# A bias row with the heads innermost, written from two partitions and read back in long runs

## The chip, the cores and the metric

One NeuronCore of a Trainium2 chip runs the whole program. The metric is the device time in microseconds of one execution; lower is better. Engines are named as in the profile: PE (TensorE), ACT (ScalarE), DVE (VectorE), POOL (GpSimd), SP (SyncE, which only issues DMAs). ACT and POOL issue DMAs as well.

## The reference

Attention with a relative position bias over batch 8, 8 heads, 576 positions and head size 64, followed by a mixture of eight low-rank adapters of which each row uses its two best.

```python
scores = scale * q @ k.T                     # scale = 1/8
n = abs(pos[:, None] - pos[None, :])
bucket = n if n < 16 else 16 + int(log(n/16)/log(8) * 15), at most 31
scores += bias_table[bucket]                 # table of 32 buckets x 8 heads
attn = softmax(scores); x = attn @ v         # rows of 8 heads x 64
logits = x @ w_gate; two best experts, softmax over the two
out = x + sum over both of w * (x @ A[e]) @ B[e]
```

The bias depends on the distance alone. From distance 128 on it is constant, and a constant falls out of the softmax. So a row of 512 numbers per head, indexed by signed distance, holds all of it, and every tile of bias is a shifted copy of this row.

## The kernel before, in words

**Tiling.** The work goes in 32 pairs of heads (8 batches x 4 pairs, pair hp holds heads hp and hp+4). A pair has five steps g: four of 128 keys against 512 queries for both heads (PE writes 128x1024 scores, ACT takes the exponential, L375 and L396), and a fifth for the 64 tail positions (L381). The first 512 positions are split as position = 4 p + j. After its steps a pair is multiplied by v (pv, L426), divided (recip and norm) and written to x. The mixture of a batch is spread over the slots of the next two batches; the tuple MIX says in which slot each of its parts is issued.

**Order.** Nothing is scheduled automatically: the order of each engine is the order of the calls. At the start the steps are reordered by START: the twelve main steps of pairs 0 to 2 come first, then their three tail steps, since these need the bias tile B. OPS lists, by step, what else is issued: ckq and pkq cast q and k, T transposes them, M makes a bias table for a pair, b multiplies the probabilities of a step by it, cv casts v, ts scores the tails, pv and rn finish a pair. SPQ, POOLQ and POOLQ2 are the orders of the SP and POOL queues at the start.

**The bias.** The table (32 x 8) is loaded by two DMAs with the heads on 8 partitions (L69 to L73). POOL subtracts the last bucket and scales (L212); gg holds per head the row of logarithms and its exponential (512 each, L208 and L236). It is filled with copies by POOL and ACT (L225 to L235), one for each bucket of several distances. ACT writes gg to a DRAM buffer g_d (L238). From there it is read back with a shift for each partition:
- Mr (L243, load_bias at L247): the exponential, for the main steps. Partition 32 j + t begins at 4 t + j; 8 heads x 384 numbers, in four DMAs on SP, one for each j. band_table (L286) turns a pair's part round into M, read at a step of -4 numbers; band_of (L402) multiplies the probabilities by it on DVE.
- MHr (L262) and Br (L256): the logarithm, for the tail steps, in two and four DMAs on POOL. tail_bias (L290) makes B4 and BT of them on POOL, which PE adds to the scores through an identity (L357, L389, L391).

All of this happens while ACT already takes exponentials, which need no bias; M and B are needed when the first pair is finished. At most eight DMAs of the hardware queues have a semaphore of their own: the next one on SP waits until the DMA eight before it has landed.

cv(0), the first cast of v, needs all four groups of v (16 DMAs of 64 KB in SPQ). On DVE it stands after M(1) and four b.

Of the kernel before, what the change touches and what calls it, by code (L numbers as in the profile page):

```python
# [10 lines left out]
FP32 = mybir.dt.float32  # L11
BF16 = mybir.dt.bfloat16
AX = mybir.AxisListType
ALU = mybir.AluOpType
ACT = mybir.ActivationFunctionType
# [12 lines left out]
def kernel(  # L28
# [14 lines left out]
    nc = tc.nc  # L43
    B, H, S, D = q.shape
    NB = bias_table.shape[0]
# [4 lines left out]
    HP = H // 2  # L50
    D1 = D + 1
    scale = 1.0 / float(np.sqrt(D))
    S4 = 512
    MW = 384
# [3 lines left out]
    cp = ctx.enter_context(tc.tile_pool(name="const", bufs=1))  # L58
    ldp = ctx.enter_context(tc.tile_pool(name="loads", bufs=2))
# [5 lines left out]
    op = ctx.enter_context(tc.tile_pool(name="outs", bufs=2))  # L65
    scp = ctx.enter_context(tc.tile_pool(name="sc_ps", bufs=2, space=PSUM))
    acp = ctx.enter_context(tc.tile_pool(name="acc_ps", bufs=4, space=PSUM))

    btT = cp.tile([H, NB], FP32, tag="btT")  # L69
    for e in range(2):  # L70
        (nc.gpsimd if e else nc.scalar).dma_start(
            out=btT.rearrange("(c e) b -> e c b", e=2)[e],
            in_=bias_table.rearrange("b (e c) -> e c b", e=2)[e])  # L73
    warm = cp.tile([128, 1], FP32, tag="warm")
    nc.vector.memset(warm, 0.0)
    fill = cp.tile([128, 512], BF16, tag="fill")
    nc.vector.memset(fill, 1.0)
    nc.scalar.activation(warm, warm, ACT.Exp)
    ident = cp.tile([128, 128], BF16, tag="ident")
    make_identity(nc, ident)  # L80

    START = ((0, 0), (0, 1), (0, 2), (0, 3), (1, 0), (1, 1), (1, 2), (1, 3), (2, 0), (2, 1),
             (2, 2), (2, 3), (0, 4), (1, 4), (2, 4))
    SPQ = (('v', 0), ('v', 1), ('M', 0, 8), ('v', 2), ('v', 3), ('kq', 0, 3), ('kq', 1, 0),
           ('kq', 1, 1), ('kq', 1, 2), ('kq', 1, 3), ('v1', 0), ('v1', 1), ('v1', 2),
           ('v1', 3))
    POOLQ = (('tl', 0, 0), ('tl', 0, 1), ('tl', 1, 0), ('tl', 1, 1), ('MH', 0), ('MH', 1),
             ('Br', 0), ('Br', 1), ('Br', 2), ('Br', 3))
    POOLQ2 = (('vt', 0), ('vt', 1), ('B', 0), ('B', 1), ('B', 2))
    OPS = {0: (('ckq', 1), ('T', 1)),  # L90
           3: (('ckq', 2),),
           4: (('T', 2),),
# [3 lines left out]
           8: (('M', 0),),  # L96
           9: (('b', 0, 0), ('b', 0, 1)),
           10: (('M', 1), ('b', 0, 2), ('b', 0, 3), ('ts', 0), ('pkq', 4, 0)),
           11: (('cv', 0), ('b', 1, 0), ('b', 1, 1)),
           12: (('M', 2), ('b', 1, 2), ('b', 1, 3), ('T', 3), ('pkq', 4, 1)),  # L100
           13: (('cv', 1), ('b', 2, 0), ('b', 2, 1), ('pv', 0, 0), ('pv', 0, 1), ('pv', 0, 2),
                ('rn', 0, 0)),
# [3 lines left out]
           17: (('pv', 2, 0), ('pv', 2, 1), ('pv', 2, 2), ('rn', 2, 0)),  # L106
           18: (('cv', 3), ('tt', 1), ('pv', 2, 3), ('pv', 2, 4), ('rn', 2, 1))}
    LAST = ((2, 'pv', 0), (2, 'pv', 1), (1, 'eh', 7), (1, 'pv', 2), (1, 'pv', 3))

    def keep_busy(n, cols=512):  # L110
        ps = acp.tile([128, 512], FP32, name="fl", tag="acc")
        for _ in range(n):
            nc.tensor.matmul(ps[:, :cols], lhsT=fill[:, 0:128], rhs=fill[:, :cols],
                             start=True, stop=True, skip_group_check=True)

    class Recorder:

# [12 lines left out]
    dve = Recorder(nc.vector)  # L130
# [9 lines left out]
    kfs, vns, vfs = {}, [], {}  # L140
# [11 lines left out]
    def load_v(b, js):  # L152
        if b not in vfs:
            vfs[b] = ldp.tile([128, 4, H, D], FP32, name="vf", tag="vf")
        vr = v[b, :, :S4, :].rearrange("h (t p j) d -> j t p h d", t=4, j=4)
        return [nc.sync.dma_start(out=vfs[b][j * 32:(j + 1) * 32, t], in_=vr[j, t])
                for j in js for t in range(4)]
# [3 lines left out]
    tls, vts = [], []  # L161
    for i in range(2):
        tl = cp.tile([128, 2, HP, 128], BF16, name=f"tl{i}", tag=f"tl{i}")
        tls.append(tl)
        vt = cp.tile([128, HP, 2 * D1], BF16, name=f"vt{i}", tag=f"vt{i}")
# [4 lines left out]
    def load_tail(b, w, e):  # L170
        sr = (k, q, v)[w][b, :, S4:, :].rearrange("(e c) p d -> e p c d", e=2)
        s = slice(e * 64, (e + 1) * 64)
        o = (tls[b % 2][s, w, :, s] if w < 2 else
             vts[b % 2][s, :, e * D1:e * D1 + D])
        nc.gpsimd.dma_start(out=o, in_=sr[e])  # L175
# [16 lines left out]
    def v_ones(eng, vt):  # L192
        eng.memset(vt[0:64, :, D:D1], 1.0)
        eng.memset(vt[64:128, :, 2 * D + 1:2 * D1], 1.0)
# [5 lines left out]
    for t in tls[:1] + vts[:1]:  # L200
# [4 lines left out]


    C = 255
    gg = cp.tile([H, 2, 512], BF16, tag="gg")  # L208
    g_sb = gg[:, 0]
    nc.gpsimd.memset(g_sb, 0.0)  # L210
    bsub = cp.tile([H, NB], FP32, tag="bsub")
    nc.gpsimd.tensor_scalar(bsub, btT, btT[:, NB - 1:NB], 1.0 / scale,  # L212
                      op0=ALU.subtract, op1=ALU.mult)
    buckets = [_bucket(d, NB) for d in range(256)]
    lo = 0
    runs = []
    for d in range(1, 129):
        if d == 128 or buckets[d] != buckets[lo]:
            runs.append((buckets[lo], lo, d))
            lo = d  # L220
    assert all(x == NB - 1 for x in buckets[128:])
    nsm = 0
    while runs[nsm][0] == nsm and runs[nsm][2] == nsm + 1:
        nsm += 1
    nc.gpsimd.tensor_copy(g_sb[:, C:C + nsm], bsub[:, :nsm])  # L225
    nc.gpsimd.tensor_copy(
        g_sb[:, C - nsm + 1:C],
        bass.AP(tensor=bsub.tensor, offset=bsub.offset + nsm - 1,
                ap=[bsub.ap[0], [-1, nsm - 1]]))
    for bv, lo, hi in runs[nsm:]:  # L230
        n = hi - lo
        dst = bass.AP(tensor=g_sb.tensor, offset=g_sb.offset + C - hi + 1,
                      ap=[g_sb.ap[0], [hi - 1 + lo, 2], [1, n]])
        (nc.scalar.copy if bv % 3 else nc.gpsimd.tensor_copy)(
            dst, bsub[:, bv:bv + 1].unsqueeze(2).to_broadcast((H, 2, n)))  # L235
    nc.scalar.activation(gg[:, 1], g_sb, ACT.Exp, scale=scale)  # L236
    g_d = nc.dram_tensor("g_d", (H, 2, 512), BF16, kind="Internal")
    nc.scalar.dma_start(out=g_d.ap(), in_=gg)  # L238
    cast_kq(0, 0, dve)
    cast_kq(0, 1, dve)  # L240
    gt = g_d.ap()

    Mr = cp.tile([128, H, MW], BF16, tag="Mr")  # L243
    MHr = cp.tile([128, HP, 192], BF16, tag="MHr")
    Br = cp.tile([128, H, 64], BF16, tag="Br")

    def load_bias(h0, h1):  # L247
        for j in range(4):
            nc.sync.dma_start(
                out=Mr[j * 32:(j + 1) * 32, h0:h1],  # L250
                in_=bass.AP(tensor=gt.tensor, offset=gt.offset + h0 * 1024 + 512 + j,
                            ap=[[4, 32], [1024, h1 - h0], [1, MW]]))

    alloc_kq(1)

    def load_br(j, eng):  # L256
        eng.dma_start(
            out=Br[j * 32:(j + 1) * 32],
            in_=bass.AP(tensor=gt.tensor, offset=gt.offset + 64 + j,
                        ap=[[4, 32], [1024, H], [1, 64]]))  # L260

    def load_mh(e, eng):  # L262
        eng.dma_start(
            out=MHr[e * 64:(e + 1) * 64],
            in_=bass.AP(tensor=gt.tensor, offset=gt.offset + e * 1024 + 192,
                        ap=[[1, 64], [2048, HP], [1, 192]]))

    for f, *a in SPQ:
        {"v": lambda j: load_v(0, (j,)), "M": load_bias, "kq": load_kq,
         "v1": lambda j: load_v(1, (j,)), "Br": lambda j: load_br(j, nc.sync),  # L270
         "MH": lambda e: load_mh(e, nc.sync)}[f](*a)
    for f, *a in POOLQ:
        {"tl": lambda w, e: load_tail(0, w, e), "Br": lambda j: load_br(j, nc.gpsimd),
         "MH": lambda e: load_mh(e, nc.gpsimd)}[f](*a)

# [4 lines left out]
    def at(t, off, *dims):  # L282
        return bass.AP(tensor=t.tensor, offset=t.offset + off,
                       ap=[t.ap[0]] + [list(d) for d in dims])

    def band_table(hp):  # L286
        dve.tensor_copy(M[:, 2 * hp:2 * hp + 2],
                        at(Mr, 2 * hp * MW + MW - 1, (MW, 2), (-1, 4), (-4, 96)))

    def tail_bias(n):  # L290
        if n == 0:
            return nc.gpsimd.tensor_copy(
                B4[:, :, 0:128].rearrange("p c (j u) -> p c j u", j=4),
                at(MHr, 191, (192, HP), (-1, 4), (-4, 32)))
        if n == 1:
            return nc.gpsimd.tensor_copy(BT.rearrange("p c (e t) -> p c e t", e=2),
                                         at(MHr, 63, (192, HP), (0, 2), (-1, 64)))
        nc.gpsimd.tensor_copy(  # L298
            B4[:, :, 128:256].rearrange("p c (e t) -> p c e t", e=2),
            at(Br, 63, (128, HP), (64, 2), (-1, 64)))  # L300

    for f, *a in POOLQ2:
        {"vt": lambda e: load_tail(0, 2, e), "B": tail_bias, "cv": cast_v}[f](*a)
    for t in tls[1:] + vts[1:]:
        nc.gpsimd.memset(t, 0.0)
    v_ones(nc.gpsimd, vts[1])
    nc.gpsimd.memset(vns[1][:, :, :, D:D1], 1.0)


    Ab = cp.tile([128, 4, ER], BF16, tag="Ab")  # L310
# [519 lines left out]
    def pool_kq(i, w):  # L830
# [2 lines left out]
    START_OPS = {  # L833
        "cv": lambda p: cast_v(p, dve), "cvp": cast_v, "M": band_table, "b": band_of,
        "tt": tail_transposes, "ts": tail_scores, "pv": pv, "rn": renorm, "T": transposes,
        "w": keep_busy, "vt": load_tail, "B": tail_bias,
        "ckq": lambda i: (cast_kq(i, 0, dve), cast_kq(i, 1, dve)), "pkq": pool_kq}

    MIX = (4, 9, 17, 19, 19, 19, 20, 20, 22, 24, 25, 27, 30, 32, 39)
    VSLOTS = ((), (5, 7, 9, 10), (5, 7, 8, 10), (8, 10, 12, 13))  # L840
    KQSLOTS = ((14, 16), (11, 13), (11, 13), ())
    TSLOTS = ((15, 16, 17, 18), (15, 16, 17, 18), (15, 16, 17, 18), (15, 16, 17, 18))
# [107 lines left out]
```

## Time and profile before

Three runs took 203.14, 203.54 and 206.69 us, median 203.54. The profiled execution took 202.09 us, of which the span of the profile is 200.3.

| | busy us | share of the span |
|---|---|---|
| PE | 176.4 | 88% |
| DVE | 164.0 | 82% |
| ACT | 165.7 | 83% |
| POOL | 101.0 | 50% |

| stage of the start | us from the span's start |
|---|---|
| table landed, POOL subtracts | 4.88 |
| first exponential of scores | 7.58 |
| gg to g_d issued by ACT, landed | 7.21, 10.63 |
| Mr issued on SP, first M table on DVE | 10.71 to 12.51, 17.91 |
| MHr and Br issued on POOL | 10.92 to 14.48 |
| B and BT made on POOL | 16.82, 17.40, 20.29 |
| v landed, cast on DVE | 22.80 |
| first multiplication by v on PE | 26.74 |

Lines of the profile name the engine, the line of the kernel, the operation and out<-in; in brackets stands the idle time of the engine before it and what ended that time. L126 is the helper through which all DVE instructions go, so these are told apart by the tile.

### The profile page before, as it was taken

What the parts mean: (1) busy time and instruction counts of PE and PEld (TensorE: products, weight loads), DVE (VectorE), ACT (ScalarE), POOL (GpSimd) and SP (SyncE); (2) the same over time, 40 slices, a digit from 0 to 9 for tenths busy, and PEclk for the clock granted to TensorE, in tenths of its full rate; (3) what the DMA queues carried; (4) which work ended last, traced back from release to release, by engine and by line L of the source; (5) the groups of instructions that cost most, each with busy time, mean ns of one, the idle gap of its engine ahead of it and who ended that gap; (6) DMA issues with size and microseconds to landing.
All of it is one profiled execution on the core that took longest, in us unless ns stands there. A gap on an engine that the chain in (4) does not pass through costs nothing.

```text
span 200.3 us, 6922 instructions
## 1 busy us (share of the span) xinstructions
PE 176.4 (88%) x2754; PEld 118.5 (59%) x2754; DVE 164.0 (82%) x446; ACT 165.7 (83%) x198; POOL 101.0 (50%) x184
## 2 busy tenths in 40 slices
PE   1785299899999999999999999999999999999980
PEld 0342177576666667766676666666666677567730
DVE  4515599999997998889988997999879987998680
ACT  2899337899979989898979898998799898999550
POOL 4783976598755457264735383446544342411000
PEclk9999759999999999999999999999999999999999
DMA  6999999899999988999999999999999946822176
GB/s 176 246 177 162 271 317 161 131 336 159 143 240 253 155 211 171 319 223 122 221 305 313 173 196 195 363 168 182 173 297 294 225 111 183 108 110 106 56 250 221
DMA packets 87060, 41.18 MB, mean 206 GB/s; under 512 B 66284, under 2 KB 83852, under 8 KB 87028
## 3 DMA queue, kind: packets, MB, share of 16 engines
q1 hardware_dynamic: 68512, 38.15, 80.2%
q0 software_dynamic: 18144, 2.18, 19.1%
q8 instruction: 21, 0.34, 0.7%
q10 hardware_dynamic: 372, 0.41, 0.7%
q14 instruction: 11, 0.09, 0.2%
HBM read 29.97 MB, written 9.45 MB: 197 GB/s over the span
## 4 chain that ended last, share of the span: by engine, by line
PE 65%; ACT 13%; DMA 9%; POOL 5%; issue 4%; DVE 0%; DVEq 0%; ACTq 0%; POOLq 0%
PE pv L426 16%; PE sc L375 15%; ACT p L396 11%; PE sc L381 8%; PE kqps L337 7%; PE zp L563 4%; DMA Br<-g_d 3%; PE dl L584 3%; DMA tl<-in_q_dram 2%; PE tps L346 2%; DMA g_d<-gg 2%; DMA btT<-in_bias_table_dram 2%; PE lp L519 1%; PE ztps L576 1%; PE tsc L355 1%
## 5 line engine op out<-in xcount | busy, mean ns | idle before, releaser
L396 ACT ACTIVATE p<-sc 128x1024 bf16<-128x1024 f32 x160 | 152.5, 1028 | 15.6 <-PE sc L381 10.5
L126 DVE TENSOR_TENSOR p<-p,M 128x512 bf16<-128x512 bf16 (+1 forms) x128 | 62.4, 509 | 0.1
L375 PE MATMUL sc<-kqT 64*128 64x512 bf16 x256 | 51.6, 402 | 7.6 <-ACT p L396 6.7
L426 PE MATMUL pv<-vn,p 128*128 128x65 bf16 x1240 | 57.6, 196 | 0.0
L426 PEld LDWEIGHTS <-p 128*128 128x128 bf16 x1364 | 48.9, 100 | 14.1 <-issue 9.3
L185 POOL CAST kqn<-qf 128x512 bf16<-128x512 f32 x29 | 18.1, 624 | 40.0 <-DVE rc L126 35.0
L126 DVE TENSOR_TENSOR x<-pv,rc 128x384 bf16<-128x384 f32 x64 | 29.0, 453 | 1.2
L185 POOL CAST kqn<-kf 128x512 bf16<-128x512 f32 x29 | 18.2, 629 | 22.6 <-DVE zT L126 6.3
L126 DVE COPY kqT<-kqps 128x1024 bf16<-128x1024 bf16 x32 | 22.0, 687 | 9.1 <-PE kqps L337 8.4
L337 PE MATMUL kqps<-ident,kqn 128*128 128x128 bf16 x256 | 21.9, 231 | 7.1 <-DVE kqn L126 4.5
L375 PEld LDWEIGHTS <-kqT 64*128 64x128 bf16 x256 | 12.9, 94 | 25.1 <-issue 17.9
L426 PE MATMUL pv<-vt,p 128*128 128x130 bf16 x124 | 27.4, 221 | 0.0
L337 PEld LDWEIGHTS <-kqn 128*128 128x128 bf16 x256 | 15.5, 102 | 15.4 <-issue 5.9
L189 POOL CAST vn<-vf 128x512 bf16<-128x512 f32 x28 | 19.3, 691 | 5.7 <-DVE rc L126 4.4
L126 DVE RECIPROCAL rc<-pv 128x6 f32<-128x6 f32 x64 | 11.6, 181 | 8.0 <-PE pv L426 7.1
L126 DVE TENSOR_TENSOR o<-dl,x 128x512 f32<-128x512 f32 x25 | 17.0, 680 | 0.4 <-PE dl L782 0.4
L381 PEld LDWEIGHTS <-kqT 128*128 128x128 bf16 x128 | 10.0, 99 | 7.6 <-issue 2.5
L381 PE MATMUL sc<-kqT,tlT 128*128 128x512 bf16 x32 | 12.3, 386 | 1.1 <-ACT p L396 1.0
L381 PE MATMUL sc<-tlT,kqT 128*128 128x128 bf16 x128 | 12.6, 221 | 0.0
L381 PE MATMUL sc<-B,ident 128*128 128x128 bf16 x64 | 9.1, 222 | 2.2 <-POOL B L298 2.2
L175 POOL DMA_DIRECT2D vt<-in_v_dram x16 | 10.1, 636 | 0.9 <-PE sc L375 0.9
L175 POOL DMA_DIRECT2D tl<-in_k_dram x16 | 9.9, 621 | 0.0
(123 smaller groups left out, 190.4 us busy)
## 6 DMA issues: line engine op xcount, KB each, us to landing
vf<-in_v_dram SPq DMA_DIRECT2D x128, 64.0 KB, 3.6
kf<-in_k_dram SPq DMA_DIRECT2D x6, 1024.0 KB, 6.8
qf<-in_q_dram SPq DMA_DIRECT2D x6, 1024.0 KB, 9.9
out_dram<-o SPq DMA_DIRECT2D x12, 512.0 KB, 5.6
kf<-in_k_dram SPq DMA_DIRECT2D x8, 256.0 KB, 4.9
qf<-in_q_dram SPq DMA_DIRECT2D x8, 256.0 KB, 4.9
out_dram<-o SPq DMA_DIRECT2D x7, 256.0 KB, 2.6
out_dram<-ot SPq DMA_DIRECT2D x7, 128.0 KB, 7.1
```

The lines of the kernel that those rows point to most:

```text
L126: self.last = f(*a, **kw)
L175: nc.gpsimd.dma_start(out=o, in_=sr[e])
L185: return (eng or nc.gpsimd).tensor_copy(o, s)
L189: return (eng or nc.gpsimd).tensor_copy(vns[b % 2][:, :, hp:H:HP, :D], vfs[b][:, :, hp:H:HP, :])
L337: nc.tensor.transpose(o, n[:, w, j], ident)
L346: nc.tensor.transpose(ps[:, w, c, :], tls[b % 2][:, w, c, :], ident)
L375: nc.tensor.matmul(sc[:, h * 512:(h + 1) * 512], lhsT=t[s, 0, g * 128:(g + 1) * 128], rhs=t[s, 1, :], start=True, stop=True)
L381: nc.tensor.matmul(o, lhsT=lhsT, rhs=rhs, start=start, stop=stop, skip_group_check=True)
L396: nc.scalar.activation(p, scs.pop(n), ACT.Exp, scale=scale)
L426: nc.tensor.matmul(o, lhsT=lhsT, rhs=rhs, start=start, stop=stop, skip_group_check=True)
L563: nc.tensor.matmul(zp[:, t - t0, :], lhsT=xT[:, 4 * t + c, :], rhs=Ab[:, c, :], start=(t == t0 and c == 0), stop=(c == 3), skip_group_chec ...
L584: nc.tensor.matmul(ps, lhsT=zT[:, t, :], rhs=Bb, start=True, stop=True)
```

## The change

The row is built with the heads innermost: gg is 512 distances x 8 heads, in 33 partitions of which 0 holds the logarithms and 32 the exponentials (1 to 31 repeat 0). The table is loaded once into 33 partitions, by one DMA on ACT. DVE does the subtraction, the scaling and the first two copies; POOL and ACT copy the buckets of several distances, the shorter on POOL. The far ends are filled by memsets, on POOL for partitions 0 to 31 and on DVE for 32. gg takes a buffer of the loads of v, which batch 1 uses later.

g_d is now two rows of 4096 numbers. Mr, MHr and Br come by one DMA each, whose runs are 384, 192 and 64 distances of all 8 heads: 6, 3 and 1 KB. MHr holds all eight heads and not four. M, B4 and BT are made of them by the same copies, which now step over the heads (by -32 or -8 numbers).

The orders change with it. On SP, M stands before the second group of v, and k and q of pair 3 before the third. On POOL, the memsets of the second buffers (ms) move from behind B to places between the DMAs, and the load of the v tails goes ahead of them. cv(0) moves behind b(1,0) and b(1,1). MIX moves five of its fifteen parts. A tile for filling matmuls, which nothing used, goes with its memset.

```diff
-    btT = cp.tile([H, NB], FP32, tag="btT")
-    for e in range(2):
-        (nc.gpsimd if e else nc.scalar).dma_start(
-            out=btT.rearrange("(c e) b -> e c b", e=2)[e],
-            in_=bias_table.rearrange("b (e c) -> e c b", e=2)[e])
+    bt = cp.tile([33, NB, H], FP32, tag="bt")
+    nc.scalar.dma_start(out=bt, in_=bass.AP(tensor=bias_table.tensor, offset=bias_table.offset,
+                                            ap=[[0, 33], [1, NB * H]]))
...
-    fill = cp.tile([128, 512], BF16, tag="fill")
-    nc.vector.memset(fill, 1.0)
...
-    SPQ = (('v', 0), ('v', 1), ('M', 0, 8), ('v', 2), ('v', 3), ('kq', 0, 3), ('kq', 1, 0),
+    SPQ = (('v', 0), ('M',), ('v', 1), ('kq', 0, 3), ('v', 2), ('v', 3), ('kq', 1, 0),
...
-    POOLQ = (('tl', 0, 0), ('tl', 0, 1), ('tl', 1, 0), ('tl', 1, 1), ('MH', 0), ('MH', 1),
-             ('Br', 0), ('Br', 1), ('Br', 2), ('Br', 3))
-    POOLQ2 = (('vt', 0), ('vt', 1), ('B', 0), ('B', 1), ('B', 2))
+    POOLQ = (('tl', 0, 0), ('tl', 0, 1), ('tl', 1, 0), ('tl', 1, 1), ('ms', 0), ('MH',),
+             ('Br',), ('vt', 0), ('vt', 1), ('ms', 1), ('ms', 2))
+    POOLQ2 = (('B', 0), ('B', 1), ('B', 2))
...
-           11: (('cv', 0), ('b', 1, 0), ('b', 1, 1)),
+           11: (('b', 1, 0), ('b', 1, 1), ('cv', 0)),
...
-    gg = cp.tile([H, 2, 512], BF16, tag="gg")
-    g_sb = gg[:, 0]
-    nc.gpsimd.memset(g_sb, 0.0)
-    bsub = cp.tile([H, NB], FP32, tag="bsub")
-    nc.gpsimd.tensor_scalar(bsub, btT, btT[:, NB - 1:NB], 1.0 / scale,
-                      op0=ALU.subtract, op1=ALU.mult)
+    NSPLIT = 8
+    gg = ldp.tile([33, 512, H], BF16, name="gg", tag="vf")
+    far = bass.AP(tensor=gg.tensor, offset=gg.offset,
+                  ap=[[gg.ap[0][0], 32], [383 * H, 2], [1, 129 * H]])
+    nc.gpsimd.memset(far, 0.0)
+    dve.memset(bass.AP(tensor=gg.tensor, offset=gg[32:33].offset,
+                       ap=[[gg.ap[0][0], 1], [383 * H, 2], [1, 129 * H]]), 1.0)
+    bd = cp.tile([33, NB, H], FP32, tag="bd")
+    tb = cp.tile([33, NB, H], BF16, tag="tb")
+    dve.tensor_tensor(bd, bt, bt[:, NB - 1:NB, :].to_broadcast((33, NB, H)), op=ALU.subtract)
+    nc.scalar.activation(tb[32:33], bd[32:33], ACT.Exp)
+    dve.tensor_scalar(tb[0:32], bd[0:32], 1.0 / scale, None, op0=ALU.mult)
...
+    dve.tensor_copy(gg[:, C:C + nsm], tb[:, :nsm])
...
-        (nc.scalar.copy if bv % 3 else nc.gpsimd.tensor_copy)(
-            dst, bsub[:, bv:bv + 1].unsqueeze(2).to_broadcast((H, 2, n)))
-    nc.scalar.activation(gg[:, 1], g_sb, ACT.Exp, scale=scale)
-    g_d = nc.dram_tensor("g_d", (H, 2, 512), BF16, kind="Internal")
-    nc.scalar.dma_start(out=g_d.ap(), in_=gg)
+        (nc.scalar.copy if n > NSPLIT else nc.gpsimd.tensor_copy)(dst, src)
+    G = 512 * H
+    g_d = nc.dram_tensor("g_d", (2, 4, G // 4), BF16, kind="Internal")
+    nc.scalar.dma_start(out=g_d.ap(), in_=bass.AP(
+        tensor=gg.tensor, offset=gg.offset,
+        ap=[[gg.ap[0][0] * 32, 2], [G // 4, 4], [1, G // 4]]))
...
-    def load_bias(h0, h1):
-        for j in range(4):
-            nc.sync.dma_start(
-                out=Mr[j * 32:(j + 1) * 32, h0:h1],
-                in_=bass.AP(tensor=gt.tensor, offset=gt.offset + h0 * 1024 + 512 + j,
-                            ap=[[4, 32], [1024, h1 - h0], [1, MW]]))
+    def load_bias(eng=nc.sync):
+        eng.dma_start(
+            out=Mr.rearrange("p x h -> p (x h)"),
+            in_=bass.AP(tensor=gt.tensor, offset=gt.offset + G,
+                        ap=[[H, 4], [4 * H, 32], [1, MW * H]]))
...
-    def load_br(j, eng):
+    def load_br(eng):
         eng.dma_start(
-            out=Br[j * 32:(j + 1) * 32],
-            in_=bass.AP(tensor=gt.tensor, offset=gt.offset + 64 + j,
-                        ap=[[4, 32], [1024, H], [1, 64]]))
-    def load_mh(e, eng):
+            out=Br.rearrange("p x h -> p (x h)"),
+            in_=bass.AP(tensor=gt.tensor, offset=gt.offset + 64 * H,
+                        ap=[[H, 4], [4 * H, 32], [1, 64 * H]]))
+    def load_mh(eng):
         eng.dma_start(
-            out=MHr[e * 64:(e + 1) * 64],
-            in_=bass.AP(tensor=gt.tensor, offset=gt.offset + e * 1024 + 192,
-                        ap=[[1, 64], [2048, HP], [1, 192]]))
+            out=MHr.rearrange("p x h -> p (x h)"),
+            in_=bass.AP(tensor=gt.tensor, offset=gt.offset + 192 * H,
+                        ap=[[HP, 2], [H, 64], [1, 192 * H]]))
...
     def band_table(hp):
         dve.tensor_copy(M[:, 2 * hp:2 * hp + 2],
-                        at(Mr, 2 * hp * MW + MW - 1, (MW, 2), (-1, 4), (-4, 96)))
+                        at(Mr, (MW - 1) * H + hp, (HP, 2), (-H, 4), (-4 * H, 96)))
...
-                at(MHr, 191, (192, HP), (-1, 4), (-4, 32)))
+                at(MHr, 191 * H, (1, HP), (-H, 4), (-4 * H, 32)))
...
-    MIX = (4, 9, 17, 19, 19, 19, 20, 20, 22, 24, 25, 27, 30, 32, 39)
+    MIX = (4, 10, 17, 19, 19, 20, 20, 22, 22, 24, 25, 27, 27, 32, 39)
```

## The prediction

> **What bounds the kernel now.** I read the page first. TensorE is busy 88% of the span, ScalarE 83%, VectorE 82%, so no engine is idle enough to blame; the 40 slices put the losses into the first 30 us, and only there does the change do much.
>
> ```profile
> span 200.3 us, 6922 instructions
> PE 176.4 (88%) x2754; PEld 118.5 (59%) x2754; DVE 164.0 (82%) x446; ACT 165.7 (83%) x198; POOL 101.0 (50%) x184
> ```
>
> Second, the windows (stretch, length, busy us of PE, PEld, DVE, ACT, POOL, then granted clock, DMA share, GB/s).
>
> ```profile
> 15.00:17.50 2.50, 1.25 (x8) 0.20 (x5) 0.65 (x1) 2.50 (x4) 1.42 (x4) 1.00 1.19 177
> 20.00:22.50 2.50, 0.77 (x8) 0.47 (x7) 0.74 (x2) 0.98 (x2) 2.21 (x3) 0.97 1.23 190
> 22.50:25.00 2.50, 0.61 (x4) 0.34 (x4) 2.19 (x4) 0.96 (x2) 2.35 (x7) 0.50 1.10 349
> 25.00:27.50 2.50, 2.23 (x24) 1.96 (x25) 2.50 (x4) 0.52 (x1) 1.60 (x3) 0.50 1.10 348
> 27.50:30.00 2.50, 2.50 (x41) 1.68 (x38) 2.46 (x6) 1.13 (x2) 1.99 (x4) 0.66 1.33 288
> ```
>
> Until 20 us ScalarE's exponentials set the pace. From 20 to 25 us TensorE and ScalarE both stand, and the clock falls to 0.50. From 25 us VectorE is full, until 37.5. So a change of this stage is worth what it moves on VectorE after 22 us. Third, the waits between 5 and 32 us, and the chain of waits (start, us, what).
>
> ```profile
> ACT p L396 <- PE sc L381: 5.1, 2, 3.5
> POOL B L298 <- DMA Br<-g_d: 2.3, 1, 2.3
> DVE M L126 <- DMA Mr<-g_d: 2.3, 1, 2.3
> PE sc L381 <- POOL B L298: 2.2, 1, 2.2
> DVE vn L126 <- DMA vf<-in_v_dram: 2.1, 1, 2.1
> ```
> ```profile
> 7.21 3.42 DMA g_d<-gg
> 13.88 6.20 DMA Br<-g_d
> 20.29 0.92 POOL B L298
> ```
>
> The bias row is written at 7.21, its copies arrive 13 us later, and B is ready at 21.2. But two things end late together. VectorE's own row is
>
> ```profile
> 22.80 0.43 DVE L126 CAST vn<-vf 128x512 bf16<-128x512 f32 x1 [2.06 <-DMA vf<-in_v_dram]
> 23.15 1.30 DVE L126 TENSOR_TENSOR p<-p,M 128x512 bf16<-128x512 bf16 x2
> 24.37 1.77 DVE L126 COPY M<-Mr 128x768 bf16<-128x768 bf16 x1
> 27.27 0.68 DVE L126 COPY kqT<-kqps 128x1024 bf16<-128x1024 bf16 x1
> 29.43 0.18 DVE L126 RECIPROCAL rc<-pv 128x6 f32<-128x6 f32 x1
> ```
>
> It waits for v at 22.80 and reaches the first division at 29.43. That instruction is my yardstick: what it is moved by, the rest of the full stretch is moved by.
>
> **The change, part by part.**
>
> *Building the row.* Removed: one table load from the POOL queue (0.89 us), the memset of fill (0.48 on VectorE), 8-row work on POOL and the exponential over 512 columns (0.63). Added on VectorE, in front of the first k cast: a memset of 2064 elements in one partition. Rows: 512 elements took 0.485 us, 4 took 0.062, so 0.83 ns each, 1.77 us, from 2.25 to 4.0. Then the subtraction and the scaling of 256 (by the 0.42 us cast of 512, some 0.3 each) and two copies, until about 5.2. The copies wait for POOL's memset and ScalarE's exponential, and behind them on VectorE stand the first k and q casts, for which TensorE waits: they stood at 3.44 and 4.59 and come at 5.2 and 5.6, so the first scores are some 1.0 us later, at about 8.0. ScalarE's first exponential stood at 7.58, held by issuing g_d, so it loses 0.45. ScalarE idles 1.53 us before 21.52 and 3.52 before 26.98: that idleness hides the 0.45. If both vanish, it counts in full. POOL now has ten copies of 48 to 128 elements; five took 0.74, and 512 elements cost 0.61 (B), so 10 x 0.13 + 0.8 = 2.1 us, from 4.9 to 7.0. g_d is issued at about 7.2 as before. It is now two rows of 8 KB: in the trace the 8-row write raises its semaphore by 8 arrivals, a 32-row load by 16, the 4-row table load from ScalarE's queue by 4. Two instead of eight writers: 0 to 0.5 us, I take 0.3, so g_d lands at 10.9 (10.63).
>
> *POOL.* Six DMAs for MHr and Br (2 x 0.63 + 4 x 0.60 = 3.7 us) become two (1.2); the memset of tl (0.95) goes ahead of them, those of vt and vn ahead of B. MHr is issued at about 11, when it was. The 4-row table load from POOL raised its semaphore by 16 arrivals, so I take POOL's loads as spread. Before, MHr landed 4.2 to 5.2 us after issue; after, about 15.5. The three B copies took 0.61 to 0.92 and read now at steps of 64, 16 and 16 bytes instead of 8, 2 and 2: at 0.92 each, B is ready at 18.3, ahead of the 19.8 at which TensorE gets there. The 2.2 us wait goes. What is late next is v and M.
>
> The skill's rule here (GPSIMD Engine Reference, Performance pitfalls) is half as much again for GpSimd reads at steps over 8 bytes; by it B would be ready at about 18.3 too, still hidden.
>
> *VectorE's M copies* read at 64 bytes instead of 8. No row has that step: between no change (0.55) and the 1.5 of the slowest B copy against the quickest (0.83). Two of four fall into the full stretch: 0 to 0.55, I take 0.3.
>
> *SP's queue.* M moves ahead of the second v row group, four DMAs become one (1.80 us of issue to 0.45), k/q of pair 3 ahead of v groups 2 and 3. SP has then only 4 v loads to issue before it waits for g_d, and is idle from 6.6 to 10.9 instead of 9.3 to 10.7; behind the wait stand 12 v loads and all of batch 1.
>
> *How quickly M arrives decides.* 768 KB in 6 KB runs; the page's rate while 1 KB runs flow alone is 348 GB/s (22 to 28 us), 2.3 us if all 16 engines share it. But its source pattern is 4 x 32 runs (outer loop of four), its destination 128 rows. The rows I have (arrivals 4, 8, 16 for outer loops of 4, 8, 32) fit "as many engines as the outer loop allows", and none has two different outer loops. On 4 engines: 196.6 KB each; at 348/16 = 21.8 GB/s it is 9.0 us, at the 4 KB packets of the out stores (159 ns) 7.6. So 2.3 to 9.0; I take four engines, since the smaller loop fits all rows, and 8.0.
>
> The skill speaks against the change in the same place (DMA: Bandwidth & Descriptors, Rules for kernel authors, "Use all 16 engines"): the slowest loop of either pattern caps the engines, so an outer size of 4 confines the copy to four. By that rule the sum is the 204.4 below; with all engines it is the 201.9 of the first rival.
>
> On four engines: issue 10.9, first packet 1.0 later as in the trace, 8.0, landing 0.95 after the last packet: 20.85 (17.9 now). In the built program the sixth v load after M waits for M's semaphore, so seven v loads are issued only from 20.85, 0.45 each, the last landing at least 2.1 later (the least v landing in the trace): 26.1. VectorE: cv 0.43, M 0.55, two p 0.95, kqT 0.69, cv 0.42, two p 0.90 (quiet rows: POOL's memsets and casts are out of the way) bring the first division to 30.05 against 29.43, +0.6. (The M tables and six p of pairs 0 and 1 fit between 20.85 and 25.) With 0.3 for the M step: +0.9.
>
> *MIX.* z moves from slot 20 to 22, away from the tail scores; one output from 30 to 27, beside another. ScalarE idles 5.7 us in six waits for the tail scores, VectorE 1.7 for the gate. The move may win up to 0.3 or lose 0.3 in each of six batches, since two 0.68 us additions now stand together on a VectorE 90% busy. I take 0.
>
> *Sum.* +0.9 on the profiled 202.09 us (span 200.3 and 1.8 around it) is 203.0; the median of the runs, 203.54, lies 1.45 above that execution, so 204.4.
>
> **The rivals.**
>
> *M spreads over 16 engines.* For it: 128 destination rows. M and MHr land by 15.5, k/q of pair 3 by 19, and v, the last in the queue, at 23.3 (12 loads x 0.62, k/q 1.5, from 14.2). The division comes at 27.5, -1.9, +0.3 for the step: 201.9. With MIX's best (-1.8) it would be 200.1. It ends on the other side of mine. It decides if M lands before about 18.
>
> *MHr is confined too,* to two engines (its source loop is 2 x 64), and shares them with M: 8 us each, 16 together, from 11.9 to 28. B is ready at 30 instead of 21.2. ScalarE's idle 5.0 us hides part: +4, 207.5; with engines of its own MHr lands at 21 and costs +1.5. Against it: the 16 arrivals of POOL's 4-row load. It decides once B is later than about 24.
>
> *The change does nothing:* v sets the end anyway, at 22.8 before and after, and only the M step and MIX are left: 203.5 plus or minus 1.
>
> **How the numbers follow.** Four engines for M 0.48, sixteen 0.28, MHr confined 0.14, nothing 0.10. The likeliest gives 204.4 us, its own range 202.9 to 206 (landing of v 25.5 to 27.5, MIX within 1). Of all, 8 in 10 lie between 200.9 and 207.4. About 2%, some 4 us, is what a measurement of this kernel tells from no change: below 199.5 lies a fifth of the sixteen-engine case and little else, 0.08; above 207.6 half of the confined case and a tail of mine, 0.14; the rest 0.78.
>
> **What would show it.** Right: M's first copy on VectorE at 20 or later with a wait for Mr, no wait of TensorE for B, the cast of v at about 26, the first division at 30. Mr landing under 5 us from issue says sixteen engines, MHr over 9 us says it is confined. First exponential near 8.0 and g_d issued near 7.2 check the row building. M copies over 0.9 us would make the step dearer than taken. The forecast is wrong if VectorE is not full from 25 us on, or if the idle share of TensorE between 60 and 180 us (116 of 120 busy now) changes by more than 2 us: then MIX did it.

## The result and the profile after

The changed kernel took 216.85, 219.49, 223.75 and 225.60 us, median 221.62, beside 203.57 for the kernel before on the same chip: 1.0725 times as long, 95% interval 1.0568 to 1.0881. It is slower; 204.4 was forecast, with 207.4 as the upper end. (The two longest runs were disturbed and are left out of the ratio; they are in the median.) The profiled execution took 219.49 us.

The page of the changed kernel: in microseconds every engine is busy about as long as before, only the span is longer. The 40 slices are 5.4 us each. PE reads 0 in the fifth and sixth (21.8 to 32.7 us), and the DMA engines, busy 9 tenths in most others, are at 5 and 3 tenths there:

```profile
span 217.7 us, 6907 instructions
PE 174.1 (80%) x2739; PEld 119.0 (55%) x2754; DVE 166.8 (77%) x450; ACT 166.4 (76%) x193; POOL 104.4 (48%) x181
...
PE   0586004877999999999999997999997999999990
...
DMA  5795535998999996989977999889999996752166
```

Four of the stretches that were shown of the kernel before (columns as there: length, PE, PEld, DVE, ACT, POOL, clock, DMA, GB/s):

```profile
20.00:22.50 2.50, 0.60 (x6) 0.44 (x5) 0.00 (x0) 0.31 (x1) 0.00 (x0) 1.00 0.26 87
22.50:25.00 2.50, 0.00 (x0) 0.00 (x0) 0.00 (x0) 0.00 (x0) 0.00 (x0) 1.00 0.70 188
25.00:27.50 2.50, 0.00 (x0) 0.00 (x0) 0.00 (x0) 0.00 (x0) 0.00 (x0) 1.00 0.53 116
27.50:30.00 2.50, 0.00 (x0) 0.00 (x0) 1.06 (x2) 0.00 (x0) 0.00 (x0) 1.00 0.27 74
```

From 22.5 to 27.5 us no engine does anything, and yet only 188 and 116 GB/s move, where the kernel before moved 349 and 348. What all wait for is not held up by a full memory path. (The clock of 1.00 is no measurement here: the first record of the clock in this trace lies at 39.1 us. TensorE's `sc<-kqT,tlT` of 128x512 took 0.63 us at 35.56, as at 25.67 in the kernel before, where 0.50 was granted; at 1.00 it took 0.38.) Among the longest waits between 5 and 50 us are POOL's for MHr and TensorE's for BT (idle time, number, longest, in us):

```profile
POOL B L300 <- DMA MHr<-g_d: 17.2, 1, 17.2
...
PE tsc L361 <- POOL BT L304: 14.6, 1, 14.6
```

The rows in order of time, with VectorE's waits for Mr and for the cast of v:

```profile
10.46 0.68 SPq L247 DMA_DIRECT2D Mr<-g_d  x1
...
11.65 1.09 POOL L261 DMA_DIRECT2D MHr<-g_d  x1
...
13.39 9.44 SPq L137 DMA_DIRECT2D kf<-in_k_dram  x1
...
23.39 12.72 SPq L146 DMA_DIRECT2D vf<-in_v_dram  x8
28.83 0.81 DVE L116 COPY M<-Mr 128x768 bf16<-128x768 bf16 x1 [11.23 <-DMA Mr<-g_d]
...
33.06 1.03 POOL L300 COPY B<-MHr 128x512 bf16<-128x512 bf16 x1 [17.16 <-DMA MHr<-g_d]
...
39.00 0.43 DVE L116 CAST vn<-vf 128x512 bf16<-128x512 f32 x1 [6.04 <-DMA kf<-in_k_dram]
...
42.65 0.20 DVE L116 RECIPROCAL rc<-pv 128x6 f32<-128x6 f32 x1
```

Mr lands 18.3 us after its issue, MHr 21.4. (The last wait is that of the v cast; it is put down to a k load that landed as it began.) SP stands 9.44 us in one issue; the last eight v loads go out from 23.39 to 36.11, before the change from 12.56 to 18.12. The first division, the yardstick of the prediction, comes at 42.65 instead of 29.43: +13.2 where +0.9 was forecast. By divisions are meant VectorE's 72 reciprocals, 64 for the pairs and 8 for the weights of the mixture. The 25th (a pair's) comes at 96.48 instead of 82.23 (+14.3), the last (the mixture's) at 208.16 instead of 190.89 (+17.3). So most of the loss is made before the first division. The stretch from the 25th to the last takes 111.7 us instead of 108.7; in the experiments below it takes 109.0 to 113.6, and two executions of one kernel lie 0.2, 1.2 and 1.5 us apart in it. How much of these 3 us is chance stays open.

### The profile page after: what moved, and what is told of

Its sections match the earlier page's. It is cut to its first block, busy times and chain, and to the rows that moved or that the text cites. A ratio compares the mean times of both kernels' runs of the same rounds, so it can differ in the third digit from the quotient of the medians.

```text
span 217.7 us, 6907 instructions
## 1 busy us (share of the span) xinstructions
PE 174.1 (80%) x2739; PEld 119.0 (55%) x2754; DVE 166.8 (77%) x450; ACT 166.4 (76%) x193; POOL 104.4 (48%) x181
## 4 chain that ended last, share of the span: by engine, by line
PE 51%; DMA 19%; ACT 10%; SPq 6%; DVE 5%; issue 4%; POOL 3%; DVEq 0%; ACTq 0%; POOLq 0%
PE pv L430 14%; PE sc L379 12%; ACT p L400 9%; DMA vf<-in_v_dram 8%; PE sc L385 6%; DMA xT<-x 6%; PE kqps L341 5%; SPq L137 5%; PE zp L567 3%; DMA tl<-in_q_dram 2%; DVE kqT L116 2%; PE dl L588 2%; PE lp L523 2%; PE tps L350 1%; SPq L146 1%
## 5 line engine op out<-in xcount | busy, mean ns | idle before, releaser
L116 DVE TENSOR_TENSOR p<-p,M 128x512 bf16<-128x512 bf16 (+1 forms) x128 | 61.3, 502 | 0.1
L430 PE MATMUL pv<-vn,p 128*128 128x65 bf16 x1240 | 56.8, 195 | 1.3 <-POOL vn L179 1.1
L430 PEld LDWEIGHTS <-p 128*128 128x128 bf16 x1364 | 48.2, 99 | 14.9 <-issue 10.8
L175 POOL CAST kqn<-qf 128x512 bf16<-128x512 f32 x29 | 19.0, 654 | 30.6 <-DVE rc L116 29.7
L175 POOL CAST kqn<-kf 128x512 bf16<-128x512 f32 x29 | 19.5, 672 | 21.8 <-DVE zT L116 6.6
L341 PE MATMUL kqps<-ident,kqn 128*128 128x128 bf16 x256 | 21.4, 231 | 6.9 <-DVE kqn L116 6.9
L179 POOL CAST vn<-vf 128x512 bf16<-128x512 f32 x28 | 18.5, 662 | 11.9 <-DMA vf<-in_v_dram 7.2
L364 ACT ACTIVATE ptl<-tsc 128x512 bf16<-128x512 f32 x8 | 4.8, 597 | 16.6 <-PE tsc L361 16.0
L361 PE MATMUL tsc<-BT,ident 128*128 128x512 bf16 x3 | 1.3, 448 | 14.6 <-POOL BT L304 14.6
L116 DVE COPY M<-Mr 128x768 bf16<-128x768 bf16 x4 | 3.3, 825 | 11.2 <-DMA Mr<-g_d 11.2
```

The costliest lines, as they stand in the source:

```text
L116: self.last = f(*a, **kw)
L175: return (eng or nc.gpsimd).tensor_copy(o, s)
L179: return (eng or nc.gpsimd).tensor_copy(vns[b % 2][:, :, hp:H:HP, :D], vfs[b][:, :, hp:H:HP, :])
L341: nc.tensor.transpose(o, n[:, w, j], ident)
L364: nc.scalar.activation(p, ps, ACT.Exp, scale=scale)
L430: nc.tensor.matmul(o, lhsT=lhsT, rhs=rhs, start=start, stop=stop, skip_group_check=True)
```

## The experiments

Two theories were set against each other. Confinement: a load runs on no more DMA engines than the smaller outer loop of its two patterns (4 for Mr and Br, 2 for MHr, POOL's loads too), and what stands behind it on these engines or in its queue is late as well. Its rival: long runs, read over and over from the same 16 KB, are slow by themselves.

**Cut all three loads along the slow loop** (runs, bytes and queues stay):

```diff
-        eng.dma_start(
-            out=Mr.rearrange("p x h -> p (x h)"),
-            in_=bass.AP(tensor=gt.tensor, offset=gt.offset + G,
-                        ap=[[H, 4], [4 * H, 32], [1, MW * H]]))
+        for j in range(4):
+            eng.dma_start(
+                out=Mr[j * 32:(j + 1) * 32].rearrange("p x h -> p (x h)"),
+                in_=bass.AP(tensor=gt.tensor, offset=gt.offset + G + j * H,
+                            ap=[[4 * H, 32], [1, MW * H]]))
```

Likewise Br in four of 32 rows, MHr in two of 64.

> The changed kernel, with its three table loads cut along the slow outer loop of their source: Mr as four loads of 32 rows, MHr as two of 64, Br as four of 32. Runs of 6, 3 and 1 KB, bytes, addresses and the place in the queues stay. Confinement (a load runs on no more engines than the smaller of its two outer loops allows; the source loops are 4, 2 and 4): each piece now has 32 or 64 in both patterns, Mr lands under 5 us after issue instead of 17, MHr under 8 us instead of 21.4, the last v load by about 24, the first division comes at 28 to 30 instead of 42.65, and the time is 201 to 205 us. Long runs themselves slow, or re-reading the same 16 KB of DRAM (the rival): landings stay near 17 and 21 us after issue, and the time stays at 217 to 221. Later row building, strided table copies or MIX as the cause: landings come early, and the time still stays above 212.

Measured 1.0178 times the kernel before (1.0108 to 1.0247), that is 207.1 for 203.5; first division 32.76. The first M copy starts at 17.78 (17.91 before the change), so long runs by themselves do not make the loads late. Of the 7.25% some 5.5 are gone, about 11 us. The expected 201 to 205 was missed: another 1.8% remain.

**Cut only Mr.**

> The changed kernel with only Mr cut into four loads of 32 rows; MHr stays confined by its loop of 2, Br by its loop of 4. Confinement: Mr lands under 5 us after issue, and MHr has its two engines almost to itself: 196.6 KB each at 21.7 GB/s is 9 us, with what Br and the v loads put there some 12 to 14 after issue, B ready near 27 to 29 instead of 36, about 4 to 7 us above the version with all three cut: 206 to 211 us. Long runs slow: 217 to 221.

Measured 1.053 (1.0465 to 1.0596). POOL's row:

```profile
11.66 1.09 POOL L262 DMA_DIRECT2D MHr<-g_d  x1
...
26.59 1.03 POOL L301 COPY B<-MHr 128x512 bf16<-128x512 bf16 x1 [10.69 <-DMA MHr<-g_d]
```

MHr lands 14.9 us after issue, as confinement to two engines had it, and a little over its 12 to 14. The time missed upwards (206 to 211 expected, 214.3 measured), because SP stood again: its last eight v loads took from 15.54 to 29.01. In the trace, MHr's semaphore gets 14 arrivals from 16.80 to 17.70 and the last two at 25.91 and 26.53. Sixteen arrivals come in any case; only two engines carry data.

**Cut only MHr and Br.**

> The changed kernel with MHr cut into two loads of 64 rows and Br into four of 32; Mr stays one load whose source loop is 4. Confinement: MHr and Br land within 9 us, B is ready near 20 to 22; Mr has four engines, 196.6 KB each at 21.7 GB/s, 9 us plus what v, MHr and Br share there: it lands at 22 to 25, as the prediction had it (20.85), with v held behind it until 26 to 28: first division 30 to 32, time 204 to 208 us. Long runs slow: 217 to 221.

Measured 1.0561 (1.0511 to 1.0611): well over the forecast.

```profile
13.27 8.62 SPq L137 DMA_DIRECT2D kf<-in_k_dram  x1
...
23.27 1.03 POOL L302 COPY B<-MHr 128x512 bf16<-128x512 bf16 x1 [6.13 <-DMA MHr<-g_d]
...
28.97 0.82 DVE L116 COPY M<-Mr 128x768 bf16<-128x768 bf16 x1 [11.38 <-DMA Mr<-g_d]
...
34.77 0.43 DVE L116 CAST vn<-vf 128x512 bf16<-128x512 f32 x1 [1.63 <-DMA vf<-in_v_dram]
```

Mr alone confined lands as late as in the changed kernel, and the first division comes at 39.24. It does sit on four engines: its semaphore's data arrivals are four (27.99 to 28.95), and a v load issued behind it gets twelve arrivals by 13.88 and the other four only from 28.36 to 29.40. But its 32 packets of 6 KB on each of them took 429 ns on average, 13.7 us, where the prediction had 250 ns, and in between these engines carry their share of v, MHr, Br and k. That share is late for everyone: MHr, though cut, needs 10.5 us. So Mr alone and MHr alone each leave most of the loss standing (1.0561 and 1.053 against 1.0178 with both cut); together they make 1.0725, less than the sum of the two.

**Exchange the loops instead of cutting**, one load each. This separates "few engines" from "one load instead of four":

```diff
-                        ap=[[H, 4], [4 * H, 32], [1, MW * H]]))
+                        ap=[[4 * H, 32], [H, 4], [1, MW * H]]))
```

(the same for Br, and `[[H, 64], [HP, 2], ...]` for MHr.)

> The changed kernel, still one load each for Mr, MHr and Br, with the two outer loops of each source exchanged (32 x 4, 64 x 2, 32 x 4 instead of 4 x 32, 2 x 64, 4 x 32). The rows of the three tables then hold other shifts, so the output is not the reference's; bytes, runs, issues and queues are the same. Confinement by the slowest loop of the source: it behaves as the version with all three cut, Mr landing 5 to 7 us after issue, MHr about 7, time 205.5 to 209 us. One load each is slow in itself, whatever its loops (the rival): Mr lands 17 and MHr 21 us after issue again, 217 to 221 us.

Measured 1.0094 (1.0043 to 1.0146), first division 29.95. The view of DMA issues (KB each, us from issue to landing), first of the changed kernel, then with the loops exchanged:

```profile
MHr<-g_d POOLq DMA_DIRECT2D x1, 384.0 KB, 21.4
...
Br<-g_d POOLq DMA_DIRECT2D x1, 128.0 KB, 20.8
```
```profile
Mr<-g_d SPq DMA_DIRECT2D x1, 768.0 KB, 5.3
MHr<-g_d POOLq DMA_DIRECT2D x1, 384.0 KB, 6.9
Br<-g_d POOLq DMA_DIRECT2D x1, 128.0 KB, 7.2
```

Nothing but the order of two loops in the source differs. This shows confinement: 21.4 us become 6.9, and MHr's sixteen arrivals now lie within 17.16 and 18.51. The Trainium skill (DMA: Bandwidth & Descriptors, Rules for kernel authors, "Use all 16 engines") has it that the slowest loop of either pattern caps the engines; these runs agree, for SP's and POOL's loads alike (5.3 and 6.9 us with 32 and 64 outside, 18.3 and 21.4 with 4 and 2).

**The order of SP's queue.** With cut loads VectorE still stood 3.63 us for v, until 28.70. The old order, first with cut loads, then with the loads as they are:

```diff
-    SPQ = (('v', 0), ('M',), ('v', 1), ('kq', 0, 3), ('v', 2), ('v', 3), ('kq', 1, 0),
+    SPQ = (('v', 0), ('v', 1), ('M',), ('v', 2), ('v', 3), ('kq', 0, 3), ('kq', 1, 0),
```

> The version with all three loads cut, and SP's queue in the order of the kernel before (v 0, v 1, M, v 2, v 3, then k and q of pair 3). In the version with all three cut, VectorE stood 3.6 us for v until 28.70, because v 1 waited behind M for the row, and k and q of pair 3 and eight of their waits stood ahead of v 2 and v 3. Order as the cause of the rest: the last v of the first cast lands at 22.5 to 24.5, the first division comes at 29.5 to 31 instead of 32.76, and the time is 203.5 to 205.5 us. Copies at wide steps as the cause of the rest (M copies 0.83 instead of 0.55 us, B copies 1.1 to 1.4 instead of 0.61 to 0.92): the time stays at 206.5 to 208.5.

> The changed kernel, its three loads as they are (confined), with SP's queue in the order of the kernel before. Confinement as the main cause, order as an addition of 3 us: MHr lands 20 us or more after issue again, and the time is 214 to 220 us. Order as the main cause: under 209.

With cut loads 1.0066 (1.0025 to 1.0106), and in a second measurement on another chip 1.0005 (0.9931 to 1.0078), a little under the 1.003 to 1.011 expected of it; by these the order costs 1.1 to 1.7%, some 2 to 3.5 us, as expected. The first division was not early, though: 32.21, not 29.5 to 31. VectorE's rows of the first of the two show what stood in the way:

```profile
20.81 2.46 DVE L116 TENSOR_TENSOR p<-p,M 128x512 bf16<-128x512 bf16 x2
23.20 1.74 DVE L116 COPY M<-Mr 128x768 bf16<-128x768 bf16 x1
24.85 3.82 DVE L116 TENSOR_TENSOR p<-p,M 128x768 bf16<-128x768 bf16 x4
28.59 0.41 DVE L116 CAST vn<-vf 128x512 bf16<-128x512 f32 x1
```

It no longer waits for v. But beside POOL's B copies and casts six multiplications take 6.28 us, and an M copy 1.74. In the second execution the division is as late (32.25) by another row: v is cast at 25.27, and VectorE then stands 2.37 us for TensorE's transposes, which wait for a cast of k that took POOL 3.85 us (0.61 when quiet). With confined loads the old order gives 1.0668 (1.0595 to 1.0741), no clear gain on 1.0725: while the loads are confined the order shows no effect.

**What the rest is.** With the loops exchanged and the old order:

> The changed kernel with the two outer loops of each source exchanged (one load each; rows of the tables hold other shifts, so the output is not the reference's) and SP's queue in the order of the kernel before. Against the version with cut loads in that order, SP spends 0.35 us on M's issue instead of 1.72, and POOL 1.2 instead of 3.1 on MHr and Br. If issuing counts: v and B come 1 to 2 us earlier, first division 30 to 31, time 203.5 to 205.5. If it does not: 205 to 207, as with cut loads.

1.0028 (0.9984 to 1.0073), first division 30.02, as forecast if issuing counts. But the interval reaches the version with cut loads, and v was cast at 25.96, between the two executions of that version (28.59 and 25.27), so that issuing is the reason is not shown. Nor is the cost of the order as clear here: with loads exchanged the new order took 1.0094 and the old 1.0028, 0.7% apart with intervals that overlap. Then the row in two halves of four heads, which halves MHr's bytes and all steps (M reads at 32 bytes, the B copies at 32, 8 and 8; loads cut, old order):

```diff
-    gg = ldp.tile([33, 512, H], BF16, name="gg", tag="vf")
+    gg = ldp.tile([33, 2, 512, HP], BF16, name="gg", tag="vf")
...
-                        at(Mr, (MW - 1) * H + hp, (HP, 2), (-H, 4), (-4 * H, 96)))
+                        at(Mr, (MW - 1) * HP + hp, (MW * HP, 2), (-HP, 4), (-4 * HP, 96)))
```

> The version with cut loads and the old SP order, with the row laid out in two halves of four heads each, the four heads innermost: Mr in two runs of 3 KB a row, Br in two of 512 B, MHr in one of 1.5 KB, which takes 192 KB instead of 384 (a half of MHr needs four heads only). The steps of the M copies fall from 64 to 32 bytes, of the B copies from 16 to 8. If the doubled bytes of MHr and the wide steps hold the rest of the loss: MHr lands about 5 us after issue instead of 7.3, the last B copy ends by 22.5 instead of 24.2, the first division comes at 29.5 to 31 instead of 32.2, and the time is 202 to 204.5 us. If the later first exponential (8.74 instead of 7.58) or something after the first 30 us holds it: 205 to 206.5, as without halves.

> The version in two halves once more, beside the one with the early casts, on one chip with the same runs of the kernel before: a ratio of 0.995 to 1.005 again. Above 1.005, the halves don't win back the last of the loss.

0.9998 (0.9952 to 1.0045) and 0.9920 (0.9874 to 0.9966) on another chip, under the 0.995 expected; first division 29.40 and 29.64. The whole loss is gone. The medians are 204.03 and 203.42 us; whether it beats the kernel before by a few tenths of a per cent is open. To part bytes from steps, the old steps alone, for M (shown) and the three B copies (other elements of the same buffers), twice, and the bytes alone:

```diff
-                        at(Mr, (MW - 1) * H + hp, (HP, 2), (-H, 4), (-4 * H, 96)))
+                        at(Mr, 2 * hp * MW + MW - 1, (MW, 2), (-1, 4), (-4, 96)))
```
```diff
-                            ap=[[HP, 64], [1, 192 * HP]]))
+                            ap=[[HP, 64], [W - 2 * W * e, 2], [1, 192 * HP]]))
```

> The version with cut loads and the old SP order, in which the M and B copies read their tables at the steps of the kernel before (8 bytes for M, 8, 2 and 2 for B); they so take other elements of the same buffers, and the output is not the reference's. Only the step is changed. If the step sets the duration: M copies 0.55 us instead of 0.83, B copies 0.61 to 0.92 where nothing runs beside them; two M copies and the B copies on the path make it 0.5 to 1.5 us: 204.5 to 205.5. If the slowness of the B copies (1.3 to 1.4) comes from VectorE running beside them: B copies stay above 1.2, time 205.3 to 206.5.

> The version that reads M and B at the old steps, once more and beside its partner. In its first profile the 25th division came at 83.04 instead of 87.12 us, but the end lay only 0.7 us earlier, since POOL stood 6.1 us for v after 140 us instead of 2.4. If the steps hold 2 us or more and that late wait is chance: 0.99 to 0.995 times its partner. If the late wait belongs to it: 0.998 to 1.005 times its partner.

> The version with cut loads and the old SP order once more, as the partner of the two kernels beside it on one chip: 1.003 to 1.011 times the kernel before, first division near 32.

> The version in two halves, with MHr loaded as 384 KB again (each of its rows fetches the run of 1.5 KB that it needs, and a second one like it into spare room). Steps as in the version in halves, bytes as in the changed kernel: if the doubled bytes of MHr hold the last 0.7 per cent, 1.004 to 1.010 times the kernel before and MHr landing about 7 us after issue; if the steps hold it, 0.992 to 1.001 as the version in halves.

| loads cut, old order, and | ratio to the kernel before | first, 25th division |
|---|---|---|
| nothing else | 1.0066 (1.0025-1.0106), 1.0005 (0.9931-1.0078) | 32.21, 87.12; 32.25, 84.28 |
| old steps | 1.0149 (1.0093-1.0206), 1.0041 (0.9995-1.0088) | 29.97, 83.04; 29.66, 82.21 |
| halves | 0.9998, 0.9920 | 29.40, 82.01; 29.64, 82.35 |
| halves, MHr at 384 KB | 1.0007 (0.9949-1.0065) | 31.71, 84.52 |

Rows of the second execution with old steps, then of its partner:

```profile
19.68 0.81 POOL L307 COPY BT<-MHr 128x512 bf16<-128x512 bf16 x1
...
20.82 0.55 DVE L116 COPY M<-Mr 128x768 bf16<-128x768 bf16 x1
```
```profile
19.61 1.72 POOL L307 COPY BT<-MHr 128x512 bf16<-128x512 bf16 x1
...
22.93 0.84 DVE L116 COPY M<-Mr 128x768 bf16<-128x768 bf16 x1
23.86 3.85 POOL L175 CAST kqn<-kf 128x512 bf16<-128x512 f32 x1 [1.28 <-DVE M L116]
...
29.61 0.69 DVE L116 COPY kqT<-kqps 128x1024 bf16<-128x1024 bf16 x1 [2.37 <-PE kqps L344]
```

The step changes the copies: M takes 0.55 instead of 0.84 where POOL is quiet, BT 0.81 instead of 1.72 beside VectorE. For M beside POOL no such rule shows: 0.96 to 1.77 us at 8 bytes (1.77 in the kernel before), 0.83 to 1.74 at 64. The first division comes 2.2 to 2.6 us earlier with the old steps, but in this pair the partner loses most of it to the cast of 3.85 us, which took 0.61 with the old steps; whether the step is behind that was not tried. The halves with MHr at 384 KB lose their division (31.71) to the same cast, at 2.13.

The times show no gain: twice the old steps came out no faster than the partner. The first, 206.5 by its ratio, lies above the 204.5 to 205.5 forecast for the steps. The second lies at 1.0036 times its partner, in the range that was expected if POOL's late wait belongs to the version; but the partner had a late wait too, 6.4 us, where its first execution had 2.4. From 140 to 185 us POOL waits 2.4 to 6.4 us for v in all these executions, and the two of the partner's kernel take 109.0 and 110.2 us from the 25th division to the last. Such differences cover the term. The halves with MHr at 384 KB fall in the range forecast for the steps, yet the interval holds that for the bytes as well. So the split of the last 0 to 0.7% into steps and bytes is not settled.

**MIX alone, and the first exponential.** First the kernel before with the new MIX:

```diff
-    MIX = (4, 9, 17, 19, 19, 19, 20, 20, 22, 24, 25, 27, 30, 32, 39)
+    MIX = (4, 10, 17, 19, 19, 20, 20, 22, 22, 24, 25, 27, 27, 32, 39)
```

> The kernel before with only the changed MIX (z from slot 20 to 22, one output from 30 to 27). The prediction took 0, within 1.8 us either way: 203.5. If MIX carries a good part of the loss, the time is 206 or more.

0.9972 (0.9923 to 1.0020): MIX costs nothing that can be measured. Then the version in halves with the first casts early:

```diff
-    dve.memset(bass.AP(tensor=gg.tensor, offset=gg[32:33].offset,
+    nc.gpsimd.memset(bass.AP(tensor=gg.tensor, offset=gg[32:33].offset,
...
+    cast_kq(0, 0, dve)
     dve.tensor_tensor(bd, bt, bt[:, NB - 1:NB, :].to_broadcast((33, NB, H)), op=ALU.subtract)
```

> The version in two halves, with the first k and q casts ahead of the row's pieces on VectorE and the memset of the exponential's partition on POOL, which stands idle 2.4 us before its copies. If the later first exponential costs nothing, as the prediction took it (ScalarE idles 3.10 us before 27.59): the first exponential goes from 8.74 to 7.6 us, the first division stays within 0.3 of 29.40, and the time is that of the version in halves, 203 to 204.5. If it counts: first division at 28.3 to 29, 202 to 203.

The aim was missed: the first k cast came at 4.04 and ran beside POOL's memset (1.17 us instead of 0.41), the table's pieces stood behind the casts, and the first exponential fell at 9.25, not 7.6. Time 0.9898 (0.9853 to 0.9943), against 0.9920 of its partner: half a microsecond later there costs nothing that can be measured (first division 29.96 against 29.64). What an earlier one would win stays open.

## Why the prediction was wrong, point by point

Two steps of the likeliest case failed, and the runs price each of them.

- **"So I take POOL's loads as spread"** is the first. It rested on 16 arrivals of a 4-row load from POOL. The runs show that POOL's loads give 16 arrivals whatever carries them: with only Mr cut, MHr's came 14 early and two with the data, 14.9 us after issue. MHr was on two engines, as the rule that the prediction quotes for Mr gives for a loop of 2 x 64 too. The prediction held this for a rival of 0.14, and it is what happened. With only POOL's two loads, MHr and Br, confined the kernel takes 1.053, with none 1.0178.
- **"I take four engines ... and 8.0"** is the second: four engines was right (smaller loop of 4 x 32 and 128), the size was not. The version with MHr and Br cut has Mr on four engines and POOL's loads spread, as the likeliest case had them. It was forecast 0.9 us over the kernel before and measured 1.0561, some 11.4 us: Mr landed at 28.95 instead of 20.85, v was cast at 34.77 instead of 26.1, the first division came at 39.24 instead of 30.05. So the forecast would have been missed by some 10 us with the first step right. The 8.0 us of packets assumed 250 ns a packet and engines that do nothing else; there were 13.7 us of packets (12.0 in the changed kernel, 374 ns each) and other loads in between.
- **The price of the rival "MHr is confined too"** was wrong as well: B ready at 30 and +4. B was ready at 36.2 and the division came 13.2 later. That the two share engines was right: MHr's last arrivals in the changed kernel are 25.73, 26.51, 32.64 and 33.00, the twelve others come by 17.70, so the two engines that carry it are among Mr's four. Left out were Br on the same engines, the copies at 1.03 to 1.10 us instead of 0.92, and above all v: it lands behind Mr on four engines and is issued behind a queue that stands. (In the sixteen-engine rival the terms for v add up to 23.1, not 23.3; nothing rests on that.)
- **SP behind Mr**: the prediction let the sixth v load wait for M's semaphore, until 20.85. SP stood earlier, in the issue of k, for 9.44 us that no semaphore explains (the waits of SP's queue put 0.2 us on that line); why it stands is open. The order, which put M ahead of v 1 and k, q of pair 3 ahead of v 2, costs 1.1 to 1.7% with cut loads and 0.7%, not clear of noise, with exchanged ones; the prediction priced it inside v's landing only.
- **Row building**: k and q casts 5.68 and 6.01 (5.2 and 5.6 said), first exponential 8.73 (8.0), g_d issued at 8.11 (7.2); POOL's copies 2.59 us (2.1). But g_d landed at 10.45 (10.9 said): two writers took 2.3 us, eight had taken 3.42. So the chain kept its place, and these runs show no harm from this step.
- **M step**: +0.3 said for two copies; they took 0.80 to 0.87 each instead of 0.55, so +0.5 to 0.6, at the upper of its ends (0 to 0.55).
- **MIX at 0** held. **The yardstick** held only within some 4 us: the last division moved by 17.3 us where the first moved by 13.2, and by 0.7 where it moved by 0 (halves), but with the loops exchanged the first moved by 0.5 (29.95) and the last by 4.8 (195.66). What is lost there is lost between the first division and the 25th (86.69), and what holds it was not followed up.
- **What would show it**: "MHr over 9 us says it is confined" worked, it took 21.4. "M's first copy at 20 or later" came true (28.83), the three signs beside it did not: TensorE stood 14.6 us for BT, the cast of v came at 39.00, the division at 42.65. Of its two signs of being wrong, the one on VectorE came true: it was not full from 25 us on, but idle from 25.0 to 27.5. The one for MIX misled: TensorE is busy 112.0 of the 120 us from 60 to 180 instead of 116.1, yet MIX alone costs nothing; two executions of one kernel (cut loads, old order) read 115.8 and 113.3.

## What to carry to other kernels

Longer runs are no gain if the slowest loop of the load shrinks with them: put the loop of 32 or more outside, or cut the load along the short loop. In these runs a confined load cost more than its own time, since every load behind it has a share on those engines that waits, and the queue that issues them stood. So price all that stands behind such a load, in the main case as in the rivals.

## What the runs showed of the hardware

- Mr's packets of 6 KB took 253 and 278 ns on average with the loops exchanged, 357 to 429 on four engines, but 397 to 423 also where Mr was cut and ran on 16. So the number of engines does not settle it; what does was not tried.
- An issue on SP can stand for 9.44 us (8.62 with MHr cut) without a semaphore that it waits for; with loads that spread the same issue took 0.45 to 0.47.
- VectorE's copy of 768 elements took 0.54 to 0.56 us at a step of 8 bytes, 0.87 to 0.88 at 32 and 0.80 to 0.86 at 64 with POOL idle: a stair between 8 and 32, nothing beyond. The Trainium skill (SBUF — State Buffer, Specifications, on cachelines of 16 bytes) says that each step into a new line is paid for; these rows agree.
- POOL's copies of 512 took 0.61 to 0.64 at steps of 2 and 8 bytes with VectorE idle, 1.03 to 1.10 at 16 and 64, and up to 1.73 beside it.
